# An attention and MLP kernel: three more score groups on VectorE, unweighted exponent-bit terms, PV segments opened later, half-width matmuls

## The chip, the cores and the metric

The kernel runs on one core of a Trainium2 chip. The time is the device time of one execution in microseconds (us). A ratio here is the mean time of one kernel's fast runs over that of the other's of the same rounds, so it is not quite the ratio of the medians that are quoted.

Engines: PE is TensorE, PEld its weight loads, ACT is ScalarE, DVE is VectorE, POOL is GpSimd.

## The reference, cut to what matters

```python
x = A_x                                   # 2048 x 448, bf16
xn = layernorm(x)
qkv = xn @ wqkv                           # 16 heads of 28
p = softmax(q k^T * 28**-0.5)             # 16 x 2048 x 2048
attention = (p @ v) @ wo
g, u = xn @ w_gate, xn @ w_up             # 2048 x 1792
mlp = (gelu(g) * u) @ w_down              # gelu in its tanh form
return x + attention + mlp
```

There are 16 x 2048 x 2048 exponentials, and 2048 x 1792 values of tanh. A score tile holds 128 keys x 2 heads of 512 queries, so 512 score tiles of 128 x 1024 have to be turned into probabilities, one instruction each.

## The kernel before

The program is written by a greedy list scheduler in Python, which keeps a modelled clock for each engine and emits instructions in the order in which the model would start them. Each engine's program is its own instructions in that order. So a changed constant of the model changes no instruction, but may change the whole order.

A "quad" is 4 heads x 128 keys: two score tiles ("slots"). TensorE writes a slot's scores into one of three PSUM buffers, and usually ScalarE takes the exponential:

```python
def emit_exp(k):
    e = epool.tile([P, 2 * QT], BF16, tag="e", name="e")
    e_tiles[k] = e
    nc.scalar.activation(e[:], s_tiles.pop(k)[:], AF.Exp, scale=SCALE)
```

For some slots VectorE does the work instead. It scales the scores into `w`, and then builds four approximations of the exponential from exponent bits ("terms", an addition and a reinterpretation of the integer result as bf16). TensorE adds the four in the product with V, which is called PV here. In the kernel before, each term has its own weight, so three scaled copies of the values are needed:

```python
TERMS = ((-2.07786, 1.0), (-2.31032, 1.203125), (-2.56653, 1.4375), (-2.80693, 1.671875))
...
def emit_w(k):                              # one slot's scores, PSUM to SBUF
    ...
    nc.vector.tensor_scalar(out=w_tiles[g][1][:, 2 * i * QT : 2 * (i + 1) * QT],
        in0=s_tiles.pop(k)[:], scalar1=128.0 * SCALE * LOG2E, scalar2=None, op0=ALU.mult)
...
def emit_term(g, j):                        # one of four terms of a group (two slots)
    ...
    nc.vector.tensor_scalar(out=bits, in0=w[:], scalar1=c, scalar2=None, op0=ALU.add)
```

A group is two half quads of two different quads. Groups per head group (4 heads, one of 12 with queries 512 to 2047) and their places:

```python
D_AT = ((0, 4, 4), (8, 12, 12)), ((0, 4, 4), (5, 9, 8))
KINDS = "000000000001"                      # 12 head groups x 2 = 24 groups, 48 slots
```

PV products of four quads are summed in one PSUM bank, a "segment". Two banks (`aux`) serve segments, projections, the MLP and the output products alike. A segment is opened when its first PV pass is about to be ready and its last but one quad is. (A "pass" is four PV matmuls, one a head; "fillers" below are matmuls without use for the result, which the scheduler puts into long gaps of TensorE.)

```python
if seg_open[0] is None:
    if not tail:
        n2 = segs[b]["left"][-2][0]
        r = max([r] + [e_ready.get(k, INF) for k in (2 * n2, 2 * n2 + 1) if k not in d_slot])
    fb = min((v, k) for k, v in banks.items())
    r = max(r, fb[0])
```

The softmax here doesn't subtract the row's maximum and nothing guards it: scores larger than these inputs give would overflow.

## Time and profile before

| | before |
|---|---|
| median of 4 runs | 477.62 us |
| exponentials / tanh on ScalarE | 464 / 28 |
| score tiles / terms on VectorE | 48 / 96 |
| ScalarE, TensorE, VectorE recorded as busy | 97%, 95%, 83% |
| from first to last start of an exponential | 451.8 us of 475.2 |

The page's engine table and the timelines are in the prediction.

### The profile page before, as it was taken

How to read it: one execution, taken by the hardware profiler on the slowest of the kernel's cores; microseconds unless marked ns; L12 is line 12 of the kernel's file. 1: busy time of each engine (PE TensorE's matmuls, PEld its weight loads, DVE VectorE, ACT ScalarE, POOL GpSimd, SP SyncE). 2: the span in 40 equal slices, each digit the busy share in tenths (PEclk: the TensorE clock that was granted, in tenths of full speed). 3: DMA queues.
4: the chain of work that ended last, by engine and by line, in shares of the span. 5: the costliest groups of instructions: out<-in, count | busy, mean ns of one | idle time of the engine just before them, and what ended most of it. 6: DMA issues, size and time to landing. Idle time of an engine off the chain costs nothing.

```text
span 475.2 us, 8985 instructions
## 1 busy us (share of the span) xinstructions
PE 452.6 (95%) x3395; PEld 156.4 (33%) x3395; DVE 395.0 (83%) x701; ACT 459.3 (97%) x504; POOL 21.8 (5%) x86
## 2 busy tenths in 40 slices
PE   8999999999999999999999999999999999999994
PEld 3343333423333333333333333333333332223321
DVE  6788998896656989899998678999996789897674
ACT  4899999999999999999999999999999999999993
POOL 4502030100000000000000000000000000000000
PEclk9999999999999999999999999999999999999998
DMA  6920201100101012121200021121100112000001
GB/s 173 298 50 21 59 19 55 45 20 21 42 2 41 30 51 61 27 73 38 60 20 2 1 79 40 41 61 57 42 1 2 39 40 80 0 3 1 1 2 39
DMA packets 41051, 20.69 MB, mean 44 GB/s; under 512 B 8240, under 2 KB 41008, under 8 KB 41008
## 3 DMA queue, kind: packets, MB, share of 16 engines
q1 hardware_dynamic: 40112, 19.68, 15.3%
q8 instruction: 26, 0.43, 0.4%
q10 hardware_dynamic: 896, 0.44, 0.3%
q14 instruction: 17, 0.14, 0.1%
HBM read 18.09 MB, written 1.84 MB: 42 GB/s over the span
## 4 chain that ended last, share of the span: by engine, by line
PE 58%; DVE 27%; ACT 7%; issue 3%; DMA 2%; POOL 2%; ACTq 0%; SPq 0%; DVEq 0%; POOLq 0%
PE st L625 15%; PE gups L444 13%; PE ot L679 12%; PE op L505 12%; ACT e L637 6%; DVE w L647 5%; PE pp L314 4%; DVE g L430 2%; DVE otsb L701 2%; DVE t L668 2%; DVE gu L435 2%; PE pv L331 2%; DMA x<-in_A_x_dram 2%; DVE gl L400 1%; DVE gl L410 1%
## 5 line engine op out<-in xcount | busy, mean ns | idle before, releaser
L637 ACT ACTIVATE e<-st 128x1024 bf16<-128x1024 f32 x464 | 433.4, 1198 | 2.1 <-PE st L625 2.0
L625 PE MATMUL st<-qT,kT 28*128 28x512 bf16 x1024 | 131.9, 382 | 5.4 <-ACT e L637 2.5
L679 PE MATMUL ot<-e,va 128*32 128x512 bf16 x928 | 87.5, 385 | 1.9 <-ACT e L637 0.8
L625 PEld LDWEIGHTS <-kT 28*128 28x128 bf16 x1024 | 40.8, 91 | 122.5 <-issue 118.8
L647 DVE TENSOR_SCALAR w<-st 128x1024 f16<-128x1024 f32 x48 | 58.4, 1219 | 7.4 <-PE st L625 7.2
L444 PE MATMUL gups<-xnT,wg 112*128 112x512 bf16 x224 | 61.3, 381 | 2.0 <-DVE otsb L701 0.7
L444 PE MATMUL gups<-xnT,wu 112*128 112x512 bf16 x224 | 60.7, 381 | 1.5 <-DVE kT L320 0.8
L505 PE MATMUL op<-wd_sb,ht 128*128 128x448 bf16 x224 | 50.1, 354 | 1.7 <-DVE otsb L701 0.6
L668 DVE TENSOR_SCALAR t<-w 128x2048 uint16<-128x2048 f16 x72 | 47.9, 680 | 0.2
L430 DVE CAST g<-gups 128x512 bf16<-128x512 f32 x56 | 38.6, 688 | 10.9 <-PE gups L444 10.7
L701 DVE TENSOR_TENSOR otsb<-ot,otsb 128x512 f32<-128x512 f32 x47 | 32.3, 687 | 11.8 <-PE ot L679 11.6
L435 DVE TENSOR_TENSOR gu<-gups,g 128x512 bf16<-128x512 f32 x56 | 38.5, 687 | 3.0 <-PE gups L444 2.7
L679 PEld LDWEIGHTS <-va 128*32 128x32 bf16 x1024 | 24.0, 94 | 47.8 <-issue 40.8
L414 ACT ACTIVATE gl<-gl 128x1024 bf16<-128x1024 bf16 x28 | 33.9, 1211 | 0.0
L444 PEld LDWEIGHTS <-wu 112*128 112x128 bf16 x224 | 19.0, 97 | 30.3 <-issue 15.9
L444 PEld LDWEIGHTS <-wg 112*128 112x128 bf16 x224 | 18.9, 97 | 30.4 <-issue 15.6
L505 PEld LDWEIGHTS <-ht 128*128 128x128 bf16 x224 | 19.3, 97 | 26.0 <-issue 12.1
L533 DVE TENSOR_TENSOR pre<-op,x 128x448 f32<-128x448 f32 x16 | 10.0, 622 | 18.4 <-PE op L505 18.3
L400 DVE TENSOR_TENSOR gl<-g 128x1024 bf16<-128x1024 bf16 x28 | 19.2, 687 | 0.3
L410 DVE TENSOR_TENSOR gl<-gl,g 128x1024 bf16<-128x1024 bf16 x28 | 19.2, 687 | 0.3
L426 DVE TENSOR_TENSOR ht<-gl,gu 128x1024 bf16<-128x1024 bf16 x28 | 19.1, 686 | 0.2
L314 PE MATMUL pp<-xnT,wq_sb 112*128 112x512 bf16 x60 | 16.8, 380 | 0.6 <-DVE otsb L697 0.5
(111 smaller groups left out, 344.3 us busy)
## 6 DMA issues: line engine op xcount, KB each, us to landing
wg<-in_B_w_gate_dram SPq DMA_DIRECT2D x28, 224.0 KB
wu<-in_B_w_up_dram SPq DMA_DIRECT2D x28, 224.0 KB
out_dram<-res SPq DMA_DIRECT2D x15, 112.0 KB
wd_sb<-in_B_w_down_dram SPq DMA_DIRECT2D x1, 1568.0 KB
x<-in_A_x_dram SPq DMA_DIRECT2D x3, 448.0 KB
den<-otsb SPq DMA_DIRECT2D x60, 2.0 KB
rr<-recb SPq DMA_DIRECT2D x60, 1.0 KB
wst<-in_A_wqkv_dram SPq DMA_DIRECT2D x2, 392.0 KB
```

The costliest lines, as they stand in the source:

```text
L314: nc.tensor.matmul(pp, lhsT=wqk[comp][:, hg, c, :], rhs=xnc(T, c), start=(c == 0), stop=(c == NDC - 1))
L414: nc.scalar.activation(st["a"][:], st["a"][:], AF.Tanh, scale=TANH_SCALE)
L430: nc.vector.tensor_copy(g[:, k, :], ps[:])
L435: nc.vector.tensor_mul(gu[:, k, :], ps[:], g[:, k, :])
L444: nc.tensor.matmul(ps[:], lhsT=w[:, c, k * P : (k + 1) * P], rhs=xnc(Q, c), start=(c == 0), stop=(c == NDC - 1),)
L505: nc.tensor.matmul(ps[:, 0:D], lhsT=l, rhs=r, start=(n == 0), stop=(n == len(seq) - 1))
L625: nc.tensor.matmul(st[:, j * QT : (j + 1) * QT], lhsT=kT[(hg, kc // 4)][32 * hh : 32 * hh + Dh, (kc % 4) * P : (kc % 4 + 1) * P], rhs=qT[( ...
L637: nc.scalar.activation(e[:], s_tiles.pop(k)[:], AF.Exp, scale=SCALE)
L647: nc.vector.tensor_scalar(out=w_tiles[g][1][:, 2 * i * QT : 2 * (i + 1) * QT], in0=s_tiles.pop(k)[:], scalar1=128.0 * SCALE * LOG2E, scala ...
L668: nc.vector.tensor_scalar(out=bits, in0=w[:], scalar1=c, scalar2=None, op0=ALU.add)
L679: nc.tensor.matmul(ot[32 * hh : 32 * hh + 32, :], lhsT=va, rhs=rhs, start=(b, hh) not in started, stop=last, tile_position=(0, 32 * hh), s ...
L701: nc.vector.tensor_add(otsb[:], ot[:], otsb[:])
```

## The change

Its intent is to shorten ScalarE's part by giving six more score tiles to VectorE, and to make room on TensorE for the rest. The core of the diff, with cuts:

```diff
-TERMS = ((-2.07786, 1.0), (-2.31032, 1.203125), (-2.56653, 1.4375), (-2.80693, 1.671875))
+TERMS = (-1.68702, -1.9965, -2.23664, -2.41204)
...
-T_SWITCH = 104
-S_TO = 445
-ACT_TO = 162
-DVE_TO = 150
+T_SWITCH = 100
+S_TO = 475
+ACT_TO = 205
+DVE_TO = 160
...
-    NE = 9
+    NE = 11
...
-    D_AT = ((0, 4, 4), (8, 12, 12)), ((0, 4, 4), (5, 9, 8))
+    D_AT = ((0, 2, 4), (8, 10, 12)), ((0, 2, 4), (5, 7, 8), (9, 11, 12)), ((0, 2, 4), (4, 6, 8))
...
-    KINDS = "000000000001"
+    KINDS = "000111000002"
...  # the two half quads of a group stand side by side in a segment
+        half = [i for i, (n, _) in enumerate(left) if 2 * n in d_slot or 2 * n + 1 in d_slot]
+        if len(half) == 2:
+            left.insert(half[0] + 1, left.pop(half[1]))
...  # a segment opens when its last quad will be ready in time
-                n2 = segs[b]["left"][-2][0]
+                n2 = segs[b]["left"][-1 - OPEN_Q][0]
                 r = max([r] + [e_ready.get(k, INF) for k in (2 * n2, 2 * n2 + 1) if k not in d_slot])
+                r -= 226 * (len(sg["left"]) - 1 - OPEN_Q) if OPEN_Q < 1 else 0
...  # half of a matmul's columns where the whole would delay scores
+                if ob[2] == "sl" and ob[0] + HALF_MM + T_SWITCH <= limit and mid[0] and ...:
+                    return ob[0], lambda: do_slot(ob[0], ob[3][1], ob[3][2], True)
...
-    JUNK_GAP = 100
+    JUNK_GAP = 600
...  # the end: which result lies in which PSUM tile
-    fins = [f0[:, 0:D], fa[:, 0:D], fa[:, QT : QT + D], None]
+    fins = [fa[:, 0:D], fa[:, QT : QT + D], f0[:, 0:D], None]
```

Cut: the scaled values are gone, an unused path for GpSimd is added, MLP starting points and some limits of the scheduler are retuned.

## The prediction

> **What bounds the kernel now.** I read the page first, then the list of instructions of the exponential's line, then the timeline of ScalarE alone, then the timelines around the longest stall and at the end. The first view is the page's engine table, the second the answer for the tile `e`:
>
> ```profile
> span 475.2 us, 8985 instructions
> PE 452.6 (95%) x3395; PEld 156.4 (33%) x3395; DVE 395.0 (83%) x701; ACT 459.3 (97%) x504; POOL 21.8 (5%) x86
> ...
> L637 ACT ACTIVATE e<-st x464: 1017/1208/1353, 13.7 to 465.5; 128x1024 bf16<-128x1024 f32 x155
> ```
>
> ScalarE (464 exponentials and 28 tanh) and TensorE both look full. The busy figures cannot decide, because instructions overlap: an exponential lasts 1208 ns but the next one starts sooner. Start-to-start times decide. From the timeline of ScalarE alone:
>
> ```profile
> 118.75 1.20 ACT L414 ACTIVATE gl<-gl 128x1024 bf16<-128x1024 bf16 x1
> 119.70 9.42 ACT L637 ACTIVATE e<-st 128x1024 bf16<-128x1024 f32 x10
> 128.74 1.31 ACT L414 ACTIVATE gl<-gl 128x1024 bf16<-128x1024 bf16 x1
> 129.69 1.28 ACT L637 ACTIVATE e<-st 128x1024 bf16<-128x1024 f32 x1
> ```
>
> Ten exponentials fill 119.70 to 128.74: 904 ns each. A tanh holds the engine 0.95 us (118.75 to 119.70; 947 ns is the median over all 28). From the first exponential's start to the last one's (13.7 to 465.5, 451.8 us) lie 463 x 0.904 + 28 x 0.947 = 445.1 us of work that cannot be compressed. So ScalarE stands still for only **6.7 us** in the whole main phase. The kernel is bound by ScalarE; its time is 13.7 us head + 445.1 + 6.7 + a tail of 9.7 us, and some 2.4 us between span and measured time (477.64 - 475.2).
>
> The 6.7 us I split by comparing each exponential's start with that of its own score matmuls: 60 late ones start 0.49 us after their scores, so they wait for TensorE (5.3 us together); the rest (1.4 us) is mostly steps of 17 ns that nothing in the change touches. The largest is one of 0.80 us:
>
> ```profile
> 445.61 2.07 ACT L637 ACTIVATE e<-st 128x1024 bf16<-128x1024 f32 x2
> ...
> 446.47 2.35 DVE L647 TENSOR_SCALAR w<-st 128x1024 f16<-128x1024 f32 x2
> ...
> 447.74 0.40 PE L625 MATMUL st<-qT,kT 28*128 28x512 bf16 x4
> 448.06 0.87 PEld L505 LDWEIGHTS <-ht 128*128 128x128 bf16 x6 [0.23 <-issue]
> 448.06 1.31 PE L505 MATMUL op<-wd_sb,ht 128*128 128x448 bf16 x6
> 448.22 1.94 ACT L637 ACTIVATE e<-st 128x1024 bf16<-128x1024 f32 x2 [0.54 <-PE st L625]
> ```
>
> Two VectorE score evictions follow each other and hold two of the three score buffers, so the next scores wait for the exponential's own buffer. One also reads here that scores lead their exponential by 0.48 us (447.74 to 448.22) and that going over from scores to another kind costs TensorE 0.10 us (448.06 less 447.74 is 0.32, where a 512-column pass takes 0.216).
>
> The end, from the timeline of the last microseconds:
>
> ```profile
> 460.92 5.74 ACT L637 ACTIVATE e<-st 128x1024 bf16<-128x1024 f32 x6
> ...
> 466.66 0.35 PE L1193 MATMUL f<-prehi,ident 128*128 128x448 bf16 x1 [0.71 <-DVE pre L558]
> ...
> 467.07 0.62 DVE L562 TENSOR_TENSOR prelo<-pre,prehi 128x448 bf16<-128x448 f32 x1
> 467.13 0.40 PE L679 MATMUL ot<-e,va 128*32 128x512 bf16 x4
> 467.62 0.68 DVE L1200 TENSOR_TENSOR otb<-ot,otsb 128x512 bf16<-128x512 f32 x1
> ```
>
> The last exponential ends at 466.66, yet its PV matmul starts at 467.13: a preload, held by a late VectorE sum, stands in front of it.
>
> **What the Trainium skill says.** "Perfetto Trace Analysis", section Identifying the Most-Contended Engine: occupancy is fair for ScalarE and VectorE and bad for TensorE. The trace agrees: by spacing, TensorE has about 10% spare (below) where its row says 95%. The same page, section Optimizing Scalar/DVE Operations, gives a ScalarE instruction about 51 ns on PSUM and 93 ns on SBUF beyond its elements. With the 1 element per cycle at 1.2 GHz of "ScalarE: Activation LUTs", What ACT_TABLE_LOAD costs, an estimate from both pages is 1024/1.2 + 51 = 904 ns and 946 ns; the trace has 904 and 947. So 904 ns is a floor, and only fewer instructions or fewer stalls help. "TensorE: Matmul & The Clock Gate", Part 3, The mechanism: small matmuls in different tiles of the array overlap with starts about 4 ns apart; four PV matmuls of four heads do so here (3 to 4 ns).
>
> **The change, part by part.**
>
> *27 groups for 24.* Each group takes two half quads (a quad is 4 heads x 128 keys) from ScalarE to VectorE. 54 score tiles go to VectorE instead of 48, so 458 exponentials for 464: 6 x 0.904 = **5.4 us** less on the bounding engine. This is the one term I am sure of. VectorE gets 6 x 1.219 (row L647) + 12 terms x 0.68 (row L668) = 15.5 us and loses the twelve scaled value tiles (12 x 0.383 = 4.6): 395.0 becomes 406 us, 86% of the shorter span. It stays beside ScalarE.
>
> *Unweighted terms, and a group's two half quads in one segment.* The remaining halves of a group's two quads use complementary heads, so they can now run beside each other. Passes of four PV matmuls: before 208 whole quads + 48 lone halves + 96 terms = 352; after 202 + 27 joined + 108 = 337. 15 x 0.22 = 3.3 us of TensorE time is saved. The PV term matmuls number 432 instead of 384.
>
> *Segments opened at their last quad.* From the instruction orders of the two builds, TensorE changes between scores, PV and the rest 660 times before and 628 after, between first and last score: 32 x 0.098 = 3.1 us saved. Filler matmuls rise from 6 to 14 (1.7 us, in gaps of over 0.6 us, so free). Summing passes, columns and transitions at the measured spacings, TensorE needs some 403 us before and 400 after, against 445 and 440 us for ScalarE. Its spare time stays the same: what it saves, the six missing exponentials take away again. None of these 6 us is on the path by itself.
>
> *Half-width matmuls.* 34 matmuls are cut in two. Their worth is at most that a score pass starts up to 0.1 us sooner in 34 places, a part of the 5.3 us.
>
> *Timing constants of the scheduler.* The old order supposes scores 455 ns ahead of their exponential; the trace has 489. The new one supposes 485. Stalls of up to 70 ns, most of the sixty by number, look like this misjudgement. New positions of the VectorE scores never put two in consecutive slots, so the 0.80 us stall should go. With 11 instead of 9 exponential buffers, a late PV pass holds ScalarE less.
>
> *Tail.* The preload goes to a score buffer, and the sum it needs is computed first of the four: about 0.4 us (467.13 becomes 466.7).
>
> Sum: -5.4 (count) -0.8 (adjacent evictions) -0.4 (tail) and, of the remaining 4.5 us of waits for scores, -1.5 by my choice, about a third, for better constants and half-widths. Six more VectorE evictions, each followed by a hurry for scores, may return 0.2. 477.64 - 7.9 = 469.7; I set **469.5 us**.
>
> **Rivals.** *TensorE takes over in a stretch.* The head groups with three such groups instead of two lie together (three in a row), and in the new instruction order 68 exponentials run there without one tanh: the MLP is pushed behind it. Counting 16 score slots at a time, the new order has stretches where TensorE's work exceeds ScalarE's (15.2 against 12.7 us in the worst; before, no stretch of 16 exceeds it by more than 0.2). For it: that count. Against: the stretch in front has 3.3 us spare, and VectorE and TensorE queues move work across. It would make 471 to 473. *VectorE becomes late there.* In those groups it has 15.5 us of score work in some 24.5 us; its sum otherwise is much as before. For it: the page has slices at 9 tenths already. Against: it waited 7.2 us for scores (L647 row), the other way round, and scores waited for it only 2.2 us. It would make 470 to 473. *The retuned order removes nearly all stalls.* Then 477.64 - 5.4 - 5.3 - 0.4 gives 466.5, the floor; 468.1 is where 2% begins, and it needs 3.7 us of the 5.3.
>
> **Range and chances.** The sure term alone with nothing else gives 472.2; a new stall of a microsecond gives 473. The floor is 466.5. The range is 467.0 to 472.8. Over 2% faster needs two thirds of all waits to go: 0.25. Slower by over 2% would need 15 us of new stalls: 0.01.
>
> **What would show it.** 458 exponentials at 904 ns start to start; ScalarE's standstill, computed as above, from 6.7 to about 4; VectorE near 406 us busy; no 0.8 us stall behind two adjacent evictions; last PV pass within 0.1 us of the last exponential's end. I am wrong if the floor itself moves (spacing other than 904), if the standstill stays at 6 or grows (TensorE or VectorE late in the three dense head groups or just after), or if the tail grows.

## The result, and the profile after

The changed kernel takes 471.11 us at the median of 4 runs (470.93 to 471.88), against 477.62 of the kernel before; the ratio is 0.9866, with a 95% interval of 0.9849 to 0.9883. That is 1.3% faster, and inside the predicted range, 1.6 us above the predicted value. A later call gave 471.19 (471.05 to 471.63) and a ratio of 0.9870.

From the page of the kernel after, its engine table and the row of the exponential; then from the answer for the tile `e`:

```profile
span 469.4 us, 9080 instructions
...
PE 449.1 (96%) x3472; PEld 160.8 (34%) x3473; DVE 404.4 (86%) x707; ACT 453.7 (97%) x498; POOL 19.7 (4%) x74
...
L614 ACT ACTIVATE e<-st 128x1024 bf16<-128x1024 f32 x458 | 426.9, 1164 | 1.8 <-PE st L602 1.8
```

```profile
L614 ACT ACTIVATE e<-st x458: 1004/1162/1352, 13.6 to 459.7; 128x1024 bf16<-128x1024 f32 x153
```

458 exponentials and 404.4 us of VectorE work (406 foretold) are as they should be. From 13.6 to 459.7 are 446.1 us. By the prediction's own sum 457 x 0.904 + 28 x 0.947 = 439.6 us of that cannot be compressed, which leaves **6.5 us** of standstill, where about 4 were foretold and 6.7 stood before. So the term that should have fallen has not. The timeline of ScalarE shows why that number was never what it seemed. The columns are start, length, engine, line, instruction and count:

```profile
121.07 1.34 ACT L405 ACTIVATE gl<-gl 128x1024 bf16<-128x1024 bf16 x1
122.01 8.64 ACT L614 ACTIVATE e<-st 128x1024 bf16<-128x1024 f32 x9
130.32 1.27 ACT L405 ACTIVATE gl<-gl 128x1024 bf16<-128x1024 bf16 x1
```

Between these two tanh lie nine exponentials. Starts: 122.01 to 130.32 is 8.31 us, 923 ns each, so something held a start up by 0.17 us. Ends: the tanh ends at 122.41, the ninth exponential at 130.65; that is 8.24 us, **916 ns each**. The same in the lines of the kernel before: the ten exponentials after 119.70 start 904 ns apart, but they end at 129.12 after a tanh that ended at 119.95, 917 ns apart. Over all pairs of neighbouring exponentials whose starts are 904 ns apart, the ends are 917 ns apart at the median before and 916 after, with nearly no spread (tenth and ninetieth percentile 916 and 918). A late start thus comes out of a lead that earlier starts have built up, at 13 ns each. The length in the record grows by 13 ns from one exponential to the next (1059, 1072, 1086, 1098, 1112 at 17 to 21 us), and falls where a start is late.

What depends on an exponential waits for its end: by the traces the score passes that waited for an exponential's buffer started 50 to 52 ns after its recorded end in the kernel before (11 places) and 51 to 53 ns in the kernel after (16), whatever lead the start had. So the span is better divided by ends: the end of the first exponential, then 0.9167 us for each further exponential and 0.935 for each tanh, then standstill, then the tail from the last exponential's end. The ends come from each instruction's start and length in the trace; 0.9167 is the mean of 120 exponentials run alone (first experiment below), 0.935 the median at the tanh of both kernels.

| us | first end | completions | standstill | tail | span |
|---|---|---|---|---|---|
| before | 14.7 | 463 x 0.9167 + 28 x 0.935 = 450.6 | 1.4 | 8.6 | 475.2 |
| after | 14.7 | 457 x 0.9167 + 28 x 0.935 = 445.1 | 1.0 | 8.6 | 469.4 |
| difference | 0.0 | -5.5 | -0.3 | 0.0 | -5.8 |

Of the 5.8 us of the span 5.5 are the six exponentials, and 0.3 are standstill. (The two profiled executions took 477.01 and 471.16 us. The timed runs of the kernel before took 0.6 us longer than its profiled one, so 0.6 of the 6.5 us between the medians lies in executions that have no trace.)

The tail did not change either, though its wait went. From the timeline of the end of the kernel after, where the last exponential ends at 460.80:

```profile
460.76 0.49 PE L653 MATMUL ot<-e,va 128*32 128x512 bf16 x4
461.29 0.69 DVE L1214 TENSOR_TENSOR otb<-ot,otsb 128x512 bf16<-128x512 f32 x1 [0.17 <-PE ot L653]
...
464.02 0.86 PE L1244 MATMUL fa<-wo_sb,on 128*128 128x448 bf16 x2 [0.52 <-DVE on L1242]
464.67 0.95 PE L1244 MATMUL f<-wo_sb,on 128*128 128x448 bf16 x2
464.91 0.53 ACT L1253 CAST res<-fa 128x448 bf16<-128x448 f32 x1 [4.11 <-PE fa L1244]
...
465.48 0.62 DVE L1251 TENSOR_TENSOR res<-fa,pre 128x448 bf16<-128x448 f32 x1 [1.18 <-ACT res L1253]
```

The last PV pass now starts with the last exponential's end (before: 0.47 us later). But the clock of TensorE was halved at 464.1 us in this execution, so the last four matmuls drag (0.48 to 0.58 us each against 0.35 to 0.36 in the kernel before, which lost its clock only behind them), and VectorE's first result now waits for ScalarE's, with which it shares the PSUM tile `fa`. In the later call the clock held until 469.0 us and the tail was 8.3 us, 0.3 shorter than before.

### The profile page after: what moved, and what is told of

Same layout as the page of the kernel before. It is cut to its first block, busy times and chain, and to the rows that moved or that the text cites. A ratio compares the mean times of both kernels' runs of the same rounds, so it can differ in the third digit from the quotient of the medians.

```text
span 469.4 us, 9080 instructions
## 1 busy us (share of the span) xinstructions
PE 449.1 (96%) x3472; PEld 160.8 (34%) x3473; DVE 404.4 (86%) x707; ACT 453.7 (97%) x498; POOL 19.7 (4%) x74
## 4 chain that ended last, share of the span: by engine, by line
PE 68%; DVE 16%; ACT 11%; issue 3%; POOL 1%; DVEq 0%; ACTq 0%; POOLq 0%
PE st L602 17%; PE gups L298 17%; PE ot L653 13%; PE op L298 13%; ACT e L614 10%; PE pp L298 3%; DVE w L624 2%; PE jt L681 2%; DVE g L422 2%; DVE gu L427 2%; DVE otsb L675 1%; DVE gl L386 1%; DVE t L645 1%; PE pv L298 1%; DVE kT L335 1%
## 5 line engine op out<-in xcount | busy, mean ns | idle before, releaser
L614 ACT ACTIVATE e<-st 128x1024 bf16<-128x1024 f32 x458 | 426.9, 1164 | 1.8 <-PE st L602 1.8
L602 PE MATMUL st<-qT,kT 28*128 28x512 bf16 x1024 | 133.8, 382 | 5.5 <-ACT e L614 4.1
L653 PE MATMUL ot<-e,va 128*32 128x512 bf16 x916 | 75.6, 382 | 1.0 <-DVE otsb L675 0.7
L624 DVE TENSOR_SCALAR w<-st 128x1024 f16<-128x1024 f32 x54 | 65.9, 1220 | 11.1 <-PE st L602 10.4
L298 PE MATMUL gups<-xnT,wu 112*128 112x512 bf16 (+1 forms) x234 | 61.1, 372 | 2.6 <-DVE gu L427 1.0
L298 PE MATMUL gups<-xnT,wg 112*128 112x512 bf16 (+1 forms) x230 | 61.2, 375 | 2.2 <-DVE gu L427 1.0
L645 DVE TENSOR_SCALAR t<-w 128x2048 uint16<-128x2048 f16 x81 | 53.6, 683 | 0.9 <-PE ot L653 0.8
L298 PE MATMUL op<-wd_sb,ht 128*128 128x448 bf16 (+1 forms) x236 | 51.5, 345 | 0.6 <-DVE pre L515 0.5
L653 PEld LDWEIGHTS <-va 128*32 128x32 bf16 x1348 | 30.6, 95 | 47.3 <-issue 33.0
L653 PE MATMUL ot<-t,va 128*32 128x512 bf16 x324 | 28.6, 385 | 0.2
```

Source lines behind the costliest of these rows:

```text
L298: nc.tensor.matmul(ps[:, sl], lhsT=lhsT, rhs=rhs[:, sl], start=start, stop=stop, skip_group_check=True)
L602: nc.tensor.matmul(st[:, j * QT : (j + 1) * QT], lhsT=kT[(hg, kc // 4)][32 * hh : 32 * hh + Dh, (kc % 4) * P : (kc % 4 + 1) * P], rhs=qT[( ...
L653: nc.tensor.matmul(ot[32 * hh : 32 * hh + 32, :], lhsT=va, rhs=rhs, start=(b, hh) not in started, stop=last, tile_position=(0, 32 * hh), s ...
```

## The experiments

Twelve runs were made, in three calls, each on another chip and with the kernel before timed beside them (medians 477.23, 477.44 and 477.69 us). Differences in us between calls are good to some tenths; the ratios are within a call. Line numbers in the lines below are those of the run's own kernel.

**1. Exponentials alone.** Behind the last real exponential, 300 more activations without anything to wait for.

```diff
+    for n, name in ((120, "dexp"), (60, "dhalf"), (60, "dwide"), (60, "dsb")):
+        for _ in range(n):
+            d = epool.tile([P, 2 * QT], BF16, tag="e", name=name)
+            ... nc.scalar.activation(d[:], dmp[:], AF.Exp, scale=SCALE)      # dexp
```

> 300 extra activations are put behind the last real exponential, with nothing to wait for: 120 exponentials of 1024 columns from PSUM, 60 of 512 columns, 60 of 512 columns with fp32 output, 60 of 1024 columns from SBUF. Theory A (ScalarE completes an exponential only every 917 ns, and the 904 ns between starts is a lead that it can hold for some 25 instructions): the first starts of the 120 are 904 ns apart with durations growing by 13 ns each, then the duration stops growing near 1.3 us and the starts fall to a mean of 917 ns; ends are 917 ns apart throughout. Theory B (904 ns is the true period, the rest is waiting for TensorE): starts and ends are 904 ns apart for all 120 and the duration stays constant.

The timeline of ScalarE, from that run:

```profile
461.56 110.10 ACT L1206 ACTIVATE dexp<-dmp 128x1024 bf16<-128x1024 f32 x120 [0.18 <-PE op L298]
570.08 30.99 ACT L1208 ACTIVATE dhalf<-dmp 128x512 bf16<-128x512 f32 x60
598.73 31.74 ACT L1210 ACTIVATE dwide<-dmp 128x512 f32<-128x512 f32 x60
627.38 59.14 ACT L1212 ACTIVATE dsb<-dms 128x1024 bf16<-128x1024 bf16 x60
...
684.13 2.82 ACT L1270 CAST res<-fa 128x448 bf16<-128x448 f32 x1
```

And the answer for the tile `dexp` (lengths in ns: least, median, greatest):

```profile
L1206 ACT ACTIVATE dexp<-dmp x120: 1017/1748/2492, 461.6 to 569.2; 128x1024 bf16<-128x1024 f32 x120
```

All starts are 904 ns apart, all ends 917 (mean 916.6), with TensorE and VectorE idle. Theory A is right in what counts, and wrong in one thing: I had expected the lead to end near 1.3 us. It grows without a limit in sight: the 120th has a length of 2.49 us, and the first of the activations from SBUF 4.02. That the ends are the real times is shown behind them. The last result's copy to SBUF is recorded with a length of 2.82 us instead of 0.53, and its store is issued at 686.97, when that ends (686.95). So the recorded starts of a ScalarE that never waits run ahead of what it does. Half the columns (`dhalf`) end every 490 ns, with starts every 477.5, so the 12 to 13 ns between the two belong to an instruction and not to its columns; fp32 output is the same; from SBUF, ends are 934 ns apart and starts 946. Theory B falls: ends 904 ns apart are not to be had. (In its main phase this run is a third execution of the changed kernel's order: standstill 1.6 us, and half clock from 314.88 to 318.29 us, which experiment 5 comes back to.)

**2. The release of a score buffer modelled later.**

```diff
-ACT_TO = 205
+ACT_TO = 314
```

> The scheduler's constant for the time from an exponential's modelled end to a released score buffer is set from 205 to 314 ns, so that start to release is 1217 ns, as the trace shows at the median. Theory B (the waits for scores are TensorE work misplaced by wrong constants): waits for scores fall from about 5 us to 2 to 3, time falls by 2 to 3 us to 468 to 469. Theory A: the waits at the start side cost little, time stays within 1 us of 471.1, whatever the waits do.

494.12 us (490.4 to 495.51), ratio 1.034. Both theories missed. The new order leaves 90 matmuls other than scores behind the last score, against 29 in the changed kernel. From the timeline of ScalarE at its end:

```profile
459.82 6.52 ACT L614 ACTIVATE e<-st 128x1024 bf16<-128x1024 f32 x7 [0.98 <-PE ot L653]
488.41 0.53 ACT L1253 CAST res<-fa 128x448 bf16<-128x448 f32 x1 [22.07 <-PE fa L1244]
```

ScalarE has ended at 466.3, and 22 us later TensorE is through with what was left over, from 481.6 on at half clock. By the division above: standstill 6.4, tail 26.5 us. So the run says nothing on the waits that it was made for. It suggests that TensorE has little time to give away: what this order leaves out beside the exponentials comes back behind them, as it does in experiments 8 and 10.

**3. 24 groups again.** All else of the change stays.

```diff
-    KINDS = "000111000002"
+    KINDS = "000000000002"
```

> The changed kernel with 24 VectorE score groups instead of 27, so 464 exponentials again, all else kept. Both theories of ScalarE: 6 exponentials more, at 917 ns 5.5 us, at 904 ns 5.4 us: about 476.6 us, that is nearly all of the gain is the count. Rival (TensorE relief, segment opening and half-width matmuls carry the gain): time stays near 471 to 473. Rival (dense head groups cost VectorE or TensorE stalls that ate a part of the gain): time rises by clearly less than 5 us.

478.72 us (478.31 to 481.74), ratio 1.0045 to the kernel before. It is 7.6 us above the changed kernel; 5.5 are the six exponentials. (By the ratios, 1.0045 against 0.9866, the distance is somewhat larger.) So without the three additional groups the rest of the change gains nothing: it is even slightly slower than the kernel before. The other 2 us are probably new standstill. The profile caught an execution of 481.74 us, 3 us above the median; in it the standstill is 6.3 us against 1.0, so an estimate for the median is 3.3. 4.1 of the 6.3 us lies in or just behind stretches at half clock. The clock row of its page:

```profile
PEclk9999999999999999999999999999999899968998
```

**4. TensorE with less to do.** A wrong result; the comparison with the reference does not notice it, so small is the part that is left out.

```diff
-                for c in range(NDC):
+                for c in (0, NDC - 1):
                     yield mm(ps[:], w[:, c, k * P : (k + 1) * P], xnc(Q, c), c == 0, c == NDC - 1, T_MM)
```

> Wrong result on purpose: each gate and up product sums two of its four contraction parts, so TensorE has 224 fewer passes of 216 ns, 48 us less of its 400 us of work. Theory B (TensorE's lack of time makes ScalarE wait some 5 us): time falls by 3 to 5 us to 466 to 468. Theory A (ScalarE's completions are the floor): the waits for scores that the trace shows may shrink, but the time falls by no more than 1 us, to 470 or above.

488.48 us (486.41 to 490.35), ratio 1.025: **slower, with 48 us of matmuls less**. Neither theory had that. TensorE ran at half clock in five stretches before the last exponential, 20.5 us in all:

```profile
PEclk9999899999999899799999999998999999999997
```

5.7 of the 15.9 us of standstill lie in or just behind these stretches. The other 10 do not; they come with the new order and are not explained by this run. As a test of capacity it fails.

**5. The changed kernel again.** No edit.

> The changed kernel once more, unaltered, beside the other runs of this call and with more rounds. Theory C (in stretches where TensorE streams for less than half of some 3.4 us its clock is halved; the changed kernel has such stretches, lowest 0.41 near 312 us, and whether one is caught depends on the execution): the executions scatter by about 1 us, 470.9 to 472, those with a lower mean granted clock being the slower ones. Rival (stable like the kernel before): scatter under 0.3 us.

471.19 us (471.05 to 471.63), ratio 0.9870 (0.9857 to 0.9884). The scatter is 0.6 us, between the 1 us expected and the rival's 0.3, and the profiled execution had the clock drop that the first one had not. The windows view of both, around it (columns: stretch, its length, busy time and count of PE, PEld, DVE, ACT and POOL, granted clock, DMA share, GB/s); first the earlier execution, then this one:

```profile
312.00:315.40 3.40, 2.40 (x12) 0.67 (x11) 3.40 (x6) 3.40 (x5) 0.00 (x0) 1.00 0.02 4
315.40:318.80 3.40, 3.14 (x24) 1.03 (x23) 3.36 (x8) 3.40 (x5) 0.00 (x0) 1.00 0.00 0
```

```profile
312.00:315.40 3.40, 2.40 (x12) 0.64 (x11) 3.40 (x6) 3.40 (x5) 0.00 (x0) 1.00 0.01 2
315.40:318.80 3.40, 3.40 (x20) 0.73 (x20) 2.65 (x6) 3.40 (x4) 0.00 (x0) 0.50 0.00 0
```

In both executions TensorE has 12 matmuls in the first stretch. Only in the second does the clock go to half in the next, which then does 20 instead of 24 and takes all of it. It cost 0.7 us of standstill (1.8 against 1.0; 0.65 of it is one late exponential right behind the stretch, at 320.5 us), and the clock came back after 3.41 us. The kernel before has no stretch like that: the smallest share of any 3.41 us in which columns stream is 0.52 there, and 0.42 here, at this place. (The share is worked out from each matmul's start and columns, 216 ns for 512.)

What decides whether the low stretch is caught can be read from the traces. In all 14 of them every change of the granted clock lies a whole number of 3.413 us windows after the first one, and that grid begins at another place in each execution (4.2 to 7.2 us after the span's start). In the first execution the stretch around 312 us falls on two windows of the grid, 310.5 to 313.9 and 313.9 to 317.4 us, which stream for 53% and 64%; in this one it fills one window, 312.0 to 315.4 us, with 42%, and the drop follows at its end. In experiment 1 it is the window from 311.5 us, with 45%, and the drop follows too. Over all traces, up to the last exponential's end, the 19 full-clock windows that a drop follows stream for 22 to 52% of their time, and none of the others for less than 46%.

**6. More fillers.**

```diff
-    JUNK_GAP = 600
+    JUNK_GAP = 100
```

> The changed kernel with the gap that calls for a filler matmul set back from 600 to 100 ns, as before the change: 27 fillers instead of 14. Theory C: no clock drop in the main phase, time 470.5 to 471.2 with less scatter, a few tenths better at most. Rival (fillers stand in the way of scores): slower by 1 us or more.

472.88 us (472.79 to 474.45), ratio 0.9915. The profiled execution has no clock drop before the last exponential, but 2.9 us of standstill instead of 1.0. Fillers did not rule drops out for all executions, it seems: the two slowest of the five, 473.93 and 474.45 us, had mean clocks of 0.993 and 0.989, the others 0.996 to 0.999; they have no trace. The rival is right: 27 fillers instead of 14 cost more than they save. The retuned filler gap is a part of the change that brings some 1.7 us, of which the diff's short description says nothing.

**7. The halved MLP with fillers.** Edits of experiments 4 and 6 together; a wrong result.

> Wrong result on purpose, as in the halved MLP run, which took 488.5 us with five clock drops, and with the filler gap at 100 ns: 104 fillers instead of 54. Theory C: the slowness of the halved MLP came from the clock drops of an idle TensorE, so with fillers the drops become few and the time falls to 470 to 475. Rival (the halved MLP is slow for its altered order): stays at 485 to 490 although the drops are gone.

490.53 us (488.96 to 492.23), ratio 1.026. The fillers did not keep the clock: 30.7 us at half clock before the last exponential, more than the 20.5 without them. The stretches of 3.41 us ahead of the drops still streamed for only 0.37 to 0.52 of their time. So the question whether the clock or the order made the halved MLP slow is not settled; of 22.0 us of standstill 13.1 lie in or just behind half-clock stretches and 8.9 do not.

**8. The old opening of segments.**

```diff
-    OPEN_Q = 0
+    OPEN_Q = 1
```

> The changed kernel with PV segments opened one quad earlier, as before the change, all else kept. In its instruction order 62 matmuls other than scores stand behind the last score matmul, against 27 in the changed kernel, so about 35 x 0.19 = 6.6 us of TensorE work is left over at the end. Theory D (TensorE is the second bound: the segment opening makes room for the shorter ScalarE time): time rises by 5 to 8 us, to 476 to 479, nearly all of it after the last exponential. Rival (the opening is worth only what it saves in transitions, off the path): within 1 us of 471.1.

488.25 us (485.73 to 490.83), ratio 1.023. The direction is theory D's, the size more than double. From the timeline of TensorE, behind the last score, with the last exponential ending at 468.88:

```profile
467.42 1.69 PE L298 MATMUL op<-wd_sb,ht 128*128 128x448 bf16 x8
469.82 2.81 PE L298 MATMUL op<-wd_sb,ht 128*128 128x448 bf16 x14 [0.72 <-DVE pre L515]
473.34 0.73 PE L298 MATMUL op<-wo_sb,on 128*128 128x448 bf16 x3 [0.72 <-DVE pre L515]
...
478.03 1.28 PE L298 MATMUL op<-wo_sb,on 128*128 128x448 bf16 x3 [0.90 <-DVE pre L540]
```

The output products of the last rows are left over, and at the end they run one after the other with VectorE's sums between them, in two PSUM banks. So a leftover matmul costs more than its 0.19 us: the tail is 20.2 instead of 8.6 us. (From 477.42 us on the clock is at half, which is a part of it.) Another 9.1 us are standstill, of which 4.1 are in and behind one half-clock stretch. (The expectation counted 27 matmuls behind the last score of the changed kernel; it has 29.)

**9. No half-width matmuls.**

```diff
-    HALF_MM = 112
+    HALF_MM = 10**6
```

> The changed kernel without half-width matmuls (a gap too short for a whole matmul stays empty). 33 matmuls other than scores then stand behind the last score, against 29. Theory D (TensorE is the second bound, and what fits beside the scores must not be left for the end): time rises by the 4 leftover matmuls, 0.8 us, plus some standstill of ScalarE from the changed order, so 472 to 475. The prediction's view (worth at most a part of 5.3 us of waits): 471 to 473. Rival (34 extra instructions cost more than they bring): faster than 471.

474.23 us (473.85 to 474.67), ratio 0.9931: 3 us slower than the changed kernel. Standstill is 1.2, as good as with them. The loss is in the tail, 10.9 instead of 8.6 us, with 33 instead of 29 matmuls left over. So what the half widths brought here was not less standstill, as the prediction had it, but output products that were done in time.

**10. More groups.** The label says 30, but the edit puts three groups into five head groups instead of three, which makes 29 and 454 exponentials.

```diff
-    KINDS = "000111000002"
+    KINDS = "010101010102"
```

> 30 VectorE score groups, the three additional ones in other head groups: 452 exponentials. By ScalarE's completions alone: 6 x 0.917 = 5.5 us less, 465.6. But 78 matmuls stand behind the last score in the instruction order, against 29: theory D expects 49 x 0.19 = 9.3 us more after the last exponential and so about 475, with TensorE and no longer ScalarE as the bound of the end.

488.83 us, one execution, state unknown. Completions fall to 441.4 us as they should, and everything else takes it back: tail 22.2 us with 78 matmuls left over, standstill 8.6. In the timeline of ScalarE a single wait makes half of that:

```profile
458.37 6.52 ACT L614 ACTIVATE e<-st 128x1024 bf16<-128x1024 f32 x7 [4.01 <-PE ot L653]
```

An exponential needs a free output buffer, and waits 4 us for the PV pass that reads it. That wait begins at 454.4 us, and TensorE was at half clock from 454.2 to 457.6: of the 8.6 us of standstill 6.3 lie in or just behind half-clock stretches, so the clock, and not only the work left over, may have made it. Theory D is right in direction; it foresaw 475.

**11 and 12. 28 groups, the end rearranged.** Two arrangements that leave 27 matmuls for the end, not counting eight fillers there, as an attempt to beat both kernels.

```diff
-    KINDS = "000111000002"
+    KINDS = "110100001002"                 # the other: "000100101102"
-    fins = [fa[:, 0:D], fa[:, QT : QT + D], f0[:, 0:D], None]
+    fins = [fa[:, 0:D], f0[:, 0:D], fa[:, QT : QT + D], None]
+    ... 3, 2 and 3 filler matmuls in the three waits of the tail
```

> An attempt at a faster kernel: 28 groups in an arrangement that leaves no more matmuls for the end than the changed kernel (27 without 8 fillers), and a tail in which the two results that ScalarE evicts share one PSUM tile and the two that VectorE evicts have their own (so VectorE need not wait for ScalarE), with 8 filler matmuls in the waits of the tail to keep TensorE's clock. Expected: last exponential 2 x 0.917 = 1.8 us earlier, the tail after it 8.6 to 8.0 us, so 468.5 to 469.5 unless the new order adds standstill; if clock drops come (56 score tiles leave TensorE no less to do), 470 to 472.

> The same with another arrangement of the four head groups that have three VectorE score groups (the second and third are not neighbours). Expected as for the first arrangement; the difference between the two shows how much of the time depends on where the schedule falls rather than on the counts: under 1 us if the counts decide, several us if clock drops and standstill do.

478.27 us (478.1 to 480.58), ratio 1.003, and 477.45 us (477.26 to 478.45), ratio 1.0001. Both fail. The tail is 8.5 and 8.4 us, so rearranging it brings nothing to speak of. Completions are 443.3 us, 1.8 fewer. The standstill is 12.2 and 9.2 us, and a few long waits of ScalarE make most of it. From the timelines of ScalarE, first arrangement, then second:

```profile
425.47 1.06 ACT L405 ACTIVATE gl<-gl 128x1024 bf16<-128x1024 bf16 x1 [5.65 <-DVE gl L386]
```

```profile
414.90 1.94 ACT L614 ACTIVATE e<-st 128x1024 bf16<-128x1024 f32 x2 [3.81 <-PE ot L653]
```

In the first, a tanh stands in ScalarE's queue whose argument VectorE has not got to, and all exponentials behind it wait for 5.65 us. In the second, it is an output buffer that a PV pass still has to read. The test that the second expectation set itself does not tell: the two are 0.8 us apart, under the 1 us that was to mean that the counts decide, but both lie 8 to 10 us above what the counts gave. So the counts alone do not give the time; a few such waits make most of the rest.

All runs but the first experiment by the same division. Standstill, half clock (the time at half clock before the last exponential's end) and tail are those of the one profiled execution, whose time stands beside the median since it can differ from it by up to 3 us:

| us | exponentials | completions | standstill | half clock | tail | profiled time | median time |
|---|---|---|---|---|---|---|---|
| before | 464 | 450.6 | 1.4 | 0 | 8.6 | 477.01 | 477.62 |
| after | 458 | 445.1 | 1.0 | 0 | 8.6 | 471.16 | 471.11 |
| after, again | 458 | 445.1 | 1.8 | 3.4 | 8.3 | 471.63 | 471.19 |
| more fillers | 458 | 445.1 | 2.9 | 0 | 8.2 | 472.85 | 472.88 |
| no half widths | 458 | 445.1 | 1.2 | 0 | 10.9 | 473.85 | 474.23 |
| 24 groups | 464 | 450.6 | 6.3 | 13.7 | 8.3 | 481.74 | 478.72 |
| old opening | 458 | 445.1 | 9.1 | 3.4 | 20.2 | 490.83 | 488.25 |
| later release | 458 | 445.1 | 6.4 | 10.2 | 26.5 | 494.65 | 494.12 |
| halved MLP | 458 | 445.1 | 15.9 | 20.5 | 8.8 | 486.41 | 488.48 |
| halved MLP, fillers | 458 | 445.1 | 22.0 | 30.7 | 8.6 | 492.23 | 490.53 |
| 28 groups, first | 456 | 443.3 | 12.2 | 6.8 | 8.5 | 480.49 | 478.27 |
| 28 groups, second | 456 | 443.3 | 9.2 | 0 | 8.4 | 477.45 | 477.45 |
| 29 groups | 454 | 441.4 | 8.6 | 10.2 | 22.2 | 488.83 | 488.83 |

## Why the prediction was right or wrong, point by point

**ScalarE is the bound: right.** Of the kernel before's span all but 1.4 us of the main phase is ScalarE completing activations.

**27 groups for 24, -5.4 us: right,** measured 5.5. The step was sound and its unit slightly off: six exponentials count 0.917 us each, not 0.904. This term is nearly the whole gain of the profiled executions. That the timed gain, 6.5 us, came nearer to the predicted 7.9 is luck: 0.6 us of it lies between timed and profiled executions of the kernel before. (The prediction's 2.4 us between span and time mixes two executions for the same reason; for one execution it is 1.8.)

**ScalarE stands still for 6.7 us, of which 5.3 are waits for TensorE: wrong, and this is the step that made the predicted value too low.** The distance between starts was taken for a floor. The floor is the distance between ends, 917 ns; it was in the same lines. By it the kernel before stood still for 1.4 us, and there was nothing like 5.3 us to win. Late starts exist in both kernels (before and after some 5 us of them, measured as in the prediction: 5.3 and 5.0), but nearly all of them only use up the lead. The agreement of 904 and 947 ns with the two pages of the Trainium skill made the false floor look confirmed. The pages' terms fit the starts exactly; experiment 1 shows that the ends go by other figures.

**-0.8 us for the adjacent evictions: right as an event, in part as a size.** That wait cost 0.65 us at the ends too and is gone; a new one of 0.33 us at 410 us and small ones offset half of it. **-1.5 us for constants, half widths and buffers: wrong;** nothing of it is seen, since what it was to be taken from did not exist. All standstill together went from 1.4 to 1.0 us.

**-0.4 us in the tail: the wait went, the time did not come.** The prediction saw the PV pass 0.47 us earlier, correctly. It did not see that VectorE's first result would wait for ScalarE's, nor that the clock may halve before the last four matmuls. In the execution in which the clock held, 0.3 us did come (8.3 us).

**"None of these 6 us is on the path by itself": right as a gain, misleading as a judgement.** The segment opening and the half widths do not shorten the time by themselves, as the run with 24 groups shows, at 478.72 us. But undone beside the 27 groups, the opening costs 17 us and the half widths 3. In this order they make the six missing exponentials payable. The prediction's summed count for TensorE, 400 us against 440, suggested a spare tenth. It hid that output products need their PSUM bank and VectorE between them, so that leftovers cost more than their length.

**The rival that TensorE takes over:** it did not happen in the changed kernel, where it was foretold for the stretch of dense head groups. In the runs with 29 groups, the old opening and the later release, TensorE's leftovers made the end (tails of 20.2 to 26.5 us). The changed kernel has the opposite trouble, and behind the dense groups: their scores start between 220.7 and 294.2 us, and in the next head group, around 312 us, TensorE is so idle that its clock halved in two of three profiled executions (0.7 us in one). The prediction did not foresee this; that the dense groups cause it is not shown. **VectorE late:** not seen; 404.4 us foretold as 406, and one wait of scores for VectorE of 0.4 us in all.

**What stays open.** The undone parts were tried with the rest of the tuned scheduler around them, so each number is the part and the disturbed order together; nearly every edit, however small, made things worse. What the opening would have brought to the kernel before was not run. Why the halved MLP has about 10 us of standstill outside of the half-clock stretches was not settled. Between 46 and 52% of a window some are followed by a drop and some are not; what decides there is open. The Trainium skill, "TensorE: Matmul & The Clock Gate", Part 1, What's actually happening, says that the activity window of about 3.4 us runs freely and does not start with the kernel. The traces agree: the windows begin 4.2 to 7.2 us after the span's start, other in each execution, and the drops last 3.41 us or multiples of it.

## What to carry to other kernels

Measure an engine's pace between the ends of its instructions as well as between the starts, and take the slower for the floor: a standstill computed from the faster one is not there to be won. When two engines are nearly full, divide the span by the completions of the binding one, its standstill and the tail; then ask of each supporting change what it leaves behind for the tail. And a second engine that gets less to do is not safe either: in this kernel it fell to half clock when it streamed for less than about half of one of the clock's own 3.41 us windows, whose place differs from execution to execution.

## What the Trainium skill lacked or had wrong

- "ScalarE: Activation LUTs", What ACT_TABLE_LOAD costs, and "Perfetto Trace Analysis", Optimizing Scalar/DVE Operations: their figures give the distance between recorded starts (904 ns for 1024 columns from PSUM, 946 from SBUF; measured 904 and 946). The ends come every 917 and 934 ns. No page says that in a stream without waits the recorded starts run ahead of the ends, here by 13 ns each, until the recorded length was 4.02 us for an activation of under 1 us.
- "TensorE: Matmul & The Clock Gate", Part 1, What's actually happening: it has the clock halve after an idle window of about 3.4 us. Here the 3.41 us windows ahead of a drop before the last exponential were not idle: they streamed columns for 22 to 52% of their time. No window of that kind that kept the clock had less than 46%. No page gives a limit.
- "Perfetto Trace Analysis", Identifying the Most-Contended Engine: that matmul busy time is a poor measure agrees (95% and 96% recorded in both kernels), but no page tells how to count what TensorE leaves over for the end; here the number of matmuls behind the last score (29 and 33) went with tails of 8.6 and 10.9 us, and 62 to 90 with 20.2 to 26.5 us.
